# Column tiles for all products but scores, zero products in idle slots, and one of three VectorE copies on GpSimd, in a kernel of two independent parts (attention and a state-space layer)

## Chip, cores and metric

One core of one Trainium2 chip. The metric is the device time of one execution in microseconds; each kernel was run several times, and its median is quoted. The core has five engines that matter here: TensorE (PE in the profile, its weight loads are PEld), ScalarE (ACT), VectorE (DVE), GpSimd (POOL) and the DMA queues. A run counts as slow when it is over 1.5% above the fastest run of the same kernel; except where a run is said to be slow, all comparisons are of the others, the fast runs.

## The reference, cut to what matters

Two independent parts, their outputs side by side. Attention has 32 query heads of 20 dimensions and one shared key and value head, over 2048 positions. The other part is a complex diagonal recurrence with projections of 640 x 640.

```python
q = (x @ wq).reshape(B, S, H, Dh).transpose(0, 2, 1, 3)        # S = 2048, H = 32, Dh = 20
k, v = x @ wk, x @ wv
p = softmax(einsum("bhqd,bkd->bhqk", q, k) * Dh ** -0.5)
o = einsum("bhqk,bkd->bhqd", p, v)                              # then @ wo
# [...] the other part: h[t] = Lam_bar * h[t-1] + (x @ B_bar.T)[t];  y = 2 Re(h @ C.T) + x * Dskip
```

The scores are 2048 tiles of 128 keys by 512 (four heads share a row of work, 64 tiles for a block). Every tile needs an exponential, and that is what costs most: ScalarE's exponentials are the costliest group on the page of the kernel before, 802.2 us.

## The kernel before

The program contains a small scheduler that runs while the program is built. Each step has an assumed duration in ns; the scheduler plays the engines against each other with these durations and so fixes the order of each engine's instructions. On the chip the order is fixed, and the engines wait for each other by semaphores.

A score tile goes one of two ways. Most go through ScalarE: scores for three or two tiles are written to PSUM, ScalarE takes the exponential of all in one instruction. Some ("VectorE tiles") go through VectorE: it reads the scores from PSUM, and writes them as 16-bit integers whose bits, read as bf16, approximate the exponential. Four versions with different shifts (0, 32, 64, 96) are needed; the first comes from PSUM (`DR<-MB` in the profile), the other three are copies of it in SBUF with a number added (`DR<-DR`).

```python
SHIFTS = ((0, 0.24037683), (32, 0.20213201), (64, 0.16997209), (96, 0.14292892))

def score(self, op, m, out, bank):                 # one score tile: 20 dimensions and one row of bounds
    # [...]
    op.fns.append(self.mm(out, p.KT[32 * j:32 * j + 21, 128 * kc:128 * kc + 128],
                          p.QT[32 * j:32 * j + 21, qb % 2, gg, :], True, True, tile_position=(32 * j, 0)))

def fill_d(self, op, m):                           # a VectorE tile
    # [...]
    first = self.dve(self.ts(p.DR[:, h.index, 0, :], bank.ap, 16256.0, 0.0, ALU.add, ALU.max), 600, deps=[op], ...)
    for k, (sh, _) in enumerate(self.SHIFTS):
        if k:
            o = self.dve(self.ts(p.DR[:, h.index, k, :], p.DR[:, h.index, 0, :], float(sh), None, ALU.add), 200,
                         deps=[first], ...)
        self.pvq[b][j].append((p.VS[:, k, kc, 0:32], kc, p.DR[:, h.index, k, :].bitcast(BF16), ...))
```

TensorE works in three shapes. Score products are row tiles: up to four products of 32 rows of the array each, side by side. Products of probabilities with values (`MB<-PR,VP` and `MB<-DR,VS`) are column tiles: four of 32 columns each. All others (projections, outputs) use the array whole. In the trace of before, the four column tiles near 170.05 us start 3 to 4 ns apart, three score products near 169.6 us 2 to 4 ns, and a group of four column tiles of 512 columns takes as long to the start of the next of its shape as one full product does: 216 ns at full clock. GpSimd does almost nothing once the constants are made: 32 copies `rdX<-rdT`, which spread out the reciprocals of the softmax sums.

Of the kernel before, what the change touches and what calls it, by code (L numbers as in the profile page):

```python
# [20 lines left out]
class Op:  # L21
# [3 lines left out]
                 "seq", "land", "dma_key", "idx", "tail")  # L25

    def __init__(self, eng, fns, dur, deps=(), prio=5, reads=(), writes=(), prev=None, gate=None, hook=None,
                 dma_key=None, land=0.0, tail=0.0):
        self.eng, self.fns, self.dur = eng, list(fns), dur
        self.deps, self.prio, self.prev = list(deps), prio, prev  # L30
        self.reads, self.writes = list(reads), list(writes)
        self.gate, self.hook = gate, hook
        self.dma_key, self.land, self.tail = dma_key, land, tail
        self.start = self.end = None
        self.seq = self.idx = 0


class Schedule:
# [7 lines left out]
    OWN = {"pe": 0.0, "act": 60.0, "dve": 55.0, "pool": 100.0}  # L46
    URGENT = 1.0

    def __init__(self):
        self.t = 0.0  # L50
        self.pending = {e: [] for e in self.ENGINES}
        self.free = {e: 0.0 for e in self.ENGINES}
        self.order = []
        self.events = []
        self.procs = []
        self.dma_free = {}
        self.n = 0
        self.sources = {e: [] for e in self.ENGINES}
        self.slack = {"pe": 60.0, "dve": 150.0}

# [40 lines left out]
    def begin(self, op, eng):  # L101
        if op.hook is not None:
            op.hook(op)
        op.start = self.t
        if op.dma_key is not None:
# [9 lines left out]
        for lag in (0.0, 55.0, 60.0, 100.0, 110.0, 130.0, 150.0, 200.0):  # L115
            self.at(op.end + lag)

    def pick(self, eng):
        best = None
# [3 lines left out]
        for src in self.sources[eng]:  # L123
            extra = src()
            if extra is not None:
                cands = cands + [extra]
        for op in cands:
# [5 lines left out]
            if r <= t + 1e-6:  # L133
                if best is None or (op.prio, op.seq) < (best.prio, best.seq):
                    best = op
            elif op.prio <= self.URGENT and (urgent is None or r < urgent):
                urgent = r
        if best is None:
            return None
        if urgent is not None and best.prio > self.URGENT and t + best.dur > urgent + self.slack.get(eng, 1e9):  # L140
            return None
# [203 lines left out]
class Build:  # L345
    CHUNKS = (3, 2)
    MISC = 2
    NPS = 5
    NDS = 4
    SHARE = 0.215  # L350

    SHIFTS = ((0, 0.24037683), (32, 0.20213201), (64, 0.16997209), (96, 0.14292892))

# [49 lines left out]
    def alloc(self, o):  # L403
# [9 lines left out]
        self.QT = sb(o, "QT", [128, 2, NGG, 512], BF16)  # L413
# [3 lines left out]
        self.DR = sb(o, "DR", [128, self.NDS, len(self.SHIFTS), 512], I16)  # L417
        self.WO4 = sb(o, "WO4", [128, NGG, 640], BF16)
        self.PR = sb(o, "PR", [128, self.NPS, 3, 512], BF16)
# [13 lines left out]
        self.lift = sb(o, "lift", [128, 2], FP32)  # L433
# [20 lines left out]
    def alloc_late(self, s):  # L454
        self.W = self.sb(s, "W", [128, NC, 2, 512], BF16)
        self.g = self.sb(s, "g", [128, 2, 2, 512], BF16)
        self.OT = self.sb(s, "OT", [128, 12, 512], BF16)
        self.LATE = [f"W{c}" for c in range(NC)] + [f"g{u}_{i}" for u in range(2) for i in range(2)] \
            + [f"OT{i}" for i in range(12)]


    def pe(self, fns, dur, **kw):
        return self.s.add("pe", fns, dur, **kw)
# [28 lines left out]

    def mm(self, out, lhsT, rhs, start, stop, **kw):
        return lambda e: e.matmul(out, lhsT=lhsT, rhs=rhs, start=start, stop=stop, **kw)  # L494

    @staticmethod
    def mmt(n, k=1):
        return n / 2.3 * 1.0 + 8.0 * k
# [10 lines left out]
    def program(self):  # L509
# [5 lines left out]
        self.evac_op, self.norm_op = {}, {}  # L515
# [7 lines left out]
        self.d_per = {}  # L523
# [16 lines left out]
        self.s.sources["pe"].append(self.d_source)  # L540

    def warm_source(self):

        if self.started or self.s.t > 40000.0:
# [3 lines left out]
                  deps=[self.zero_op], reads=["PR0"], writes=[self.pvbank.key], hook=self.warm_last)  # L548
# [4 lines left out]
    def constants(self):  # L553
# [19 lines left out]
        many("VP", [lambda e: e.memset(p.VP[:], 0.0), lambda e: e.memset(p.VP[:, :, 20:21], 1.0)], 500)  # L573
# [3 lines left out]
        for k, (_, c) in enumerate(self.SHIFTS):  # L577
            fns.append(lambda e, k=k: e.memset(p.VS[:, k, :, 20:21], hi[k]))
            fns.append(lambda e, k=k, c=c: e.memset(p.VS[:, k, :, 21:22], c - hi[k]))
        many("VS", fns, 250)  # L580
        many("maskM", [
# [22 lines left out]
                                               channel_multiplier=1)], 250)  # L604
        rows = self.dve(lambda e: e.tensor_reduce(out=p.lift[:, 0:1], in_=p.E1[:], axis=AX.X, op=ALU.add), 120,
# [147 lines left out]
    def qt_task(self, qb, gg, bank):  # L753
        p = self
        prev = None
        slot = qb % 2
        for c in range(NC):
# [3 lines left out]
                           prio=3, reads=[f"xbT{qb}", "wq4"], writes=[bank.key])  # L761
        dst = p.QT[:, slot, gg, :]
        key = f"QT{slot}_{gg}"
# [11 lines left out]
        if qb == 0 and gg == 0:  # L775
            for c in range(NC):
# [7 lines left out]
                          deps=[m, self.lift_op], reads=[bank.key, "lift"], writes=[key, "QTr0_0"], prio=0.4)  # L784
# [14 lines left out]
    def row_task(self, qb, half, bank):  # L799
        p = self  # L800
        slot = qb % 2
# [3 lines left out]
        fns = [self.mm(bank.tensor[0:32, bank.off:bank.off + 512], p.Mm[:, gg, :], p.aq[:, gg % 4, :], gg == ggs[0],  # L805
                       gg == ggs[-1]) for gg in ggs]
        prev = self.pe(fns, 4 * self.mmt(512), deps=[self.mm_op] + [self.qt_op[(qb, gg)][1] for gg in ggs] + bank.last,
                       prio=1.5, reads=["Mm"] + [f"aq{i}" for i in range(4)], writes=[bank.key])
# [4 lines left out]
        if qb == 0 and half == 0:  # L813
            lo, ng = 1, 3
        fns = [lambda e, j=j: e.dma_start(p.QT[32 * j + 20:32 * j + 21, slot, lo:lo + ng, :],
# [3 lines left out]
                                           reads=[f"brow{rs}"] + [f"QT{slot}_{gg}" for gg in range(lo, lo + ng)],  # L819
                                           writes=[f"QTr{slot}_{gg}" for gg in range(lo, lo + ng)], prio=0, land=500.0)  # L820
# [13 lines left out]
    def attention(self):  # L834
# [10 lines left out]
        while self.tile_n < NTILE:  # L845
# [14 lines left out]
            fill = self.pe([], self.mmt(512, 2), deps=deps, prio=0, hook=lambda op, i=i: self.fill(op, i))  # L860
            self.next_fill = fill
            k += 1

    def fill(self, op, i):
# [7 lines left out]
        extra = None  # L872
        if self.want_d():
            tiles.append(self.tile_n)
            self.tile_n += 1
            extra = min(tiles, key=lambda m: self.d_per.get((m // 64, m % 4), 0))
            tiles.remove(extra)
# [4 lines left out]
        if extra is not None:  # L882
            self.fill_d(op, extra)
        op.reads = sorted(set(op.reads))
        op.dur = self.mmt(512, len(op.fns))
        dst = p.PR[:, h.index, 0:n, :]
        ex = self.act(lambda e: e.activation(dst, t[:, 0:512 * n], ACT.Exp, scale=1.0 / UNIT), 0.833 * 512 * n + 93,  # L887
# [12 lines left out]
    def score(self, op, m, out, bank):  # L900
# [5 lines left out]
        op.fns.append(self.mm(out, p.KT[32 * j:32 * j + 21, 128 * kc:128 * kc + 128],  # L906
                              p.QT[32 * j:32 * j + 21, qb % 2, gg, :], True, True, tile_position=(32 * j, 0)))
        op.reads += [f"KT{kc // 4}", f"QT{qb % 2}_{gg}", f"QTr{qb % 2}_{gg}"]
# [3 lines left out]
    def want_d(self):  # L912
        s = self.s
        if self.tile_n >= NTILE - 8 or self.d_count + 1 > self.SHARE * (self.tile_n - 16):
            return False
        if self.d_bank() is None:
            return False
        h = self.dhold[self.ndhold % self.NDS]
        return not h.taken or (h.left == 0 and s.done(h.users))

    def d_source(self):

        f = self.next_fill
        if f is None or f.start is None and f.deps and self.d_count == 0:
            return None
        if f.start is None:
            r = self.s.ready(f)
            if r is not None and r < self.s.t + self.ALONE:
                return None
        b = self.tile_n // 64  # L930
        if not self.started or not self.want_d() or not self.block_ready(b):
# [5 lines left out]
        def hook(op):  # L937
            self.tile_n += 1
            self.fill_d(op, self.tile_n - 1)
            op.reads = sorted(set(op.reads))  # L940
        return Op("pe", [], self.mmt(512, 1), prio=0.95, hook=hook)

    next_fill = None
    ALONE = 450.0

    def d_bank(self):
        s = self.s
        for b in self.free_banks:
            if all(o.end is not None and s.seen(o, "pe") <= s.t for o in b.last):
                return b  # L950
        return None
# [6 lines left out]
    def fill_d(self, op, m):  # L958

        p = self  # L960
        bank = self.d_bank()
# [4 lines left out]
        self.d_per[(m // 64, m % 4)] = self.d_per.get((m // 64, m % 4), 0) + 1  # L966
# [4 lines left out]
        first = self.dve(self.ts(p.DR[:, h.index, 0, :], bank.ap, 16256.0, 0.0, ALU.add, ALU.max), 600, deps=[op],  # L971
                         reads=[bank.key], writes=[k0], prio=0.5)
        self.s.spawn(self.d_give(bank, first))
        for k, (sh, _) in enumerate(self.SHIFTS):
            key = f"DR{h.index}_{k}"
            o = first
            if k:
                o = self.dve(self.ts(p.DR[:, h.index, k, :], p.DR[:, h.index, 0, :], float(sh), None, ALU.add), 200,
                             deps=[first], reads=[k0], writes=[key], prio=0.55)
# [3 lines left out]
    def pv_source(self):  # L983
# [23 lines left out]
        prio = 0.9 if tight else 2.0  # L1007
        return Op("pe", [], self.mmt(512, len(group)), prio=prio, hook=lambda op: self.pv(op, b, group))
# [5 lines left out]
    def pv(self, op, b, group):  # L1014
        p = self
        bank = self.pvbank
        for j, e in group:
            lhs, kc, rhs, key, ex, h, vk = e
# [20 lines left out]
    def norm_task(self, b, bank):  # L1039
# [3 lines left out]
        ot = b % 12  # L1043
        m1 = self.pe([self.mm(bank.cols(4 * i, 4 * i + 4), src[:, 128 * i:128 * i + 128], p.E1[:], True, True)
                      for i in range(4)], 4 * 65, deps=[self.evac_op[b], self.c_op["E1"]] + bank.last, prio=1.6,
                     reads=[f"pvsb{slot}", "E1"], writes=[bank.key])

        def rc(e):
            with p.nc.allow_low_precision("bf16 reciprocal of softmax denominator"):
                return e.reciprocal(p.rdT[:, slot, :], bank.cols(0, 16))  # L1050
        r = self.dve(rc, 230, deps=[m1], reads=[bank.key], writes=[f"rdT{slot}"], prio=1.2)
        spread = bass.AP(tensor=p.rdT, offset=16 * slot, ap=[[32, 128], [1, 16], [0, 32]])
        x = self.pool(lambda e: e.tensor_copy(p.rdX[:, slot, :, :], spread), 700, deps=[r], reads=[f"rdT{slot}"],  # L1053
                      writes=[f"rdX{slot}"], prio=1)
        fns = [self.mm(bank.cols(128 * i, 128 * i + 128),
                       p.rdX[:, slot, 4 * i:4 * i + 4, :].rearrange("p j d -> p (j d)"), p.ident[:], True, True)
               for i in range(4)]
        m2 = self.pe(fns, 4 * 65, deps=[x, self.c_op["ident"]], prio=1.6, reads=[f"rdX{slot}", "ident"],
                     writes=[bank.key])
        d = self.dve(self.tt(p.OT[:, ot, :], src, bank.ap, ALU.mult), 630, deps=[m2],  # L1060
# [406 lines left out]
```

## Time and profile before

| | before |
|---|---|
| median of the runs | 985.05 us (982.81 to 987.18) |
| PE, ACT, DVE, POOL busy | 93%, 83%, 76%, 3% of the span |
| mean granted TensorE clock | 0.833 |
| VectorE tiles | 337 of 2048 |

First the busy time of the engines, and two rows of the span cut in 40 slices: the busy share of ACT in tenths (9 is 90% or more) and the clock that TensorE was granted, in tenths of full speed.

```profile
PE 908.5 (93%) x6555; PEld 262.0 (27%) x6555; DVE 741.0 (76%) x1899; ACT 813.4 (83%) x699; POOL 32.2 (3%) x66
...
ACT  3597789988777999977979999899798979688992
...
PEclk8987679966557999976969999799697868689987
```

PE looks full, but part of that is a low clock: a score product takes 385 ns at full clock and 602 at half (medians). The 52 intervals in the trace have the clock at 1.0 or at 0.5, nothing else. After the first 35 us, 321 us are at 0.5, and in the slices where the clock is at 5 or 6, ACT is mostly at 8, 7 or 6.

The chain that ended last, by engine:

```profile
PE 65%; DVE 19%; ACT 11%; issue 3%; DMA 1%; ACTq 0%; POOL 0%; POOLq 0%; DVEq 0%
```

The groups of instructions that the argument needs: line, engine, operation, out<-in, shapes and count, then busy time and mean ns of one, then the idle time before them and what ended it. "21\*128" is the part of the array that a product claims, rows by columns.

```profile
L887 ACT ACTIVATE PR<-SC 128x1536 bf16<-128x1536 f32 (+1 forms) x685 | 802.2, 1244 | 124.9 <-PE SC L494 71.8
...
L494 PE MATMUL SC<-QT,KT 21*128 21x512 bf16 x1711 | 303.7, 439 | 36.7 <-ACT PR L887 20.9
L506 DVE TENSOR_SCALAR DR<-MB 128x512 int16<-128x512 f32 x337 | 230.8, 687 | 121.7 <-PE MB L494 110.7
...
L505 DVE TENSOR_SCALAR DR<-DR 128x512 int16<-128x512 int16 x1011 | 233.5, 288 | 9.8
...
L1053 POOL COPY rdX<-rdT 128x512 bf16<-128x512 bf16 x32 | 22.3, 698 | 916.7 <-DVE rdT L1050 916.7
```

The three copies of a VectorE tile take 288 ns each, and overlap a little. In the timeline of VectorE (start, duration, both in us):

```profile
start us, us, engine line op out<-in xcount [idle before <-releaser]
405.20 0.69 DVE L506 TENSOR_SCALAR DR<-MB 128x512 int16<-128x512 f32 x1 [1.27 <-PE MB L494]
405.92 0.70 DVE L505 TENSOR_SCALAR DR<-DR 128x512 int16<-128x512 int16 x3
406.54 0.68 DVE L506 TENSOR_SCALAR DR<-MB 128x512 int16<-128x512 f32 x1
407.25 0.70 DVE L505 TENSOR_SCALAR DR<-DR 128x512 int16<-128x512 int16 x3
```

One tile is 0.69 for the step out of PSUM and 0.70 for three copies. GpSimd and VectorE did disturb each other once in a while. Here are VectorE and then GpSimd, near 622 us:

```profile
622.51 1.12 DVE L501 TENSOR_TENSOR u<-prod 128x512 bf16<-128x512 bf16 x2
```

```profile
622.65 0.71 POOL L1053 COPY rdX<-rdT 128x512 bf16<-128x512 bf16 x1 [27.84 <-DVE rdT L1050]
```

Two VectorE products that take 439 ns on average span 1.12 us: the second, begun under GpSimd's copy, took 829 ns, and the copy 706 where its median is 613.

### The profile page before, as it was taken

The page shows a single profiled execution, that of the slowest core. Times are in us where ns is not written, and L with a number is a line of the kernel's source. Part 1 is how long each engine was busy: PE and PEld are TensorE (multiplying, and loading weights), DVE is VectorE, ACT ScalarE, POOL GpSimd, SP SyncE. Part 2 cuts the span into 40 slices and gives each one's busy share as a digit, 9 for nine tenths or more (in the row PEclk, how much of TensorE's full clock was granted, in tenths as well). Part 3 has the DMA queues.
Part 4 walks back from the last instruction along what each step waited for, and adds up shares of the span by engine and source line. Part 5 has one row for each costly group of instructions (what it writes and reads, how often), then busy time and mean ns, then how long its engine had stood idle before and what let it go on. Part 6 is the DMA issues. An engine that isn't in the chain of part 4 may idle for free.

```text
span 978.6 us, 16125 instructions
## 1 busy us (share of the span) xinstructions
PE 908.5 (93%) x6555; PEld 262.0 (27%) x6555; DVE 741.0 (76%) x1899; ACT 813.4 (83%) x699; POOL 32.2 (3%) x66
## 2 busy tenths in 40 slices
PE   7889999999899999999899999989999999998997
PEld 2322222222123322222233322222332322223323
DVE  6987678978775588876956797799576868688672
ACT  3597789988777999977979999899798979688992
POOL 4000000000000000000000000000000000000000
PEclk8987679966557999976969999799697868689987
DMA  9740000000000010000000100000000000000000
GB/s 164 118 87 1 1 2 1 1 1 2 2 1 6 23 38 12 7 1 1 2 6 17 34 11 8 11 1 1 5 14 12 1 11 6 6 6 1 17 12 27
DMA packets 49147, 16.63 MB, mean 17 GB/s; under 512 B 43572, under 2 KB 49072, under 8 KB 49072
## 3 DMA queue, kind: packets, MB, share of 16 engines
q1 hardware_dynamic: 44480, 14.72, 7.1%
q10 hardware_dynamic: 4592, 0.88, 0.7%
q8 instruction: 52, 0.85, 0.4%
q14 instruction: 23, 0.19, 0.1%
HBM read 1.69 MB, written 5.24 MB: 7 GB/s over the span
## 4 chain that ended last, share of the span: by engine, by line
PE 65%; DVE 19%; ACT 11%; issue 3%; DMA 1%; ACTq 0%; POOL 0%; POOLq 0%; DVEq 0%
PE MB L494 47%; PE SC L494 18%; ACT PR L887 11%; DVE DR L506 7%; DVE DR L505 6%; DVE prod L501 1%; DMA vec<-in_A_Dskip_dram 1%; DVE pvsb L1032 1%; DVE stg L1098 1%; DVE u L501 0%; DVE g L1255 0%; DVE W L501 0%; DVE fr L506 0%; DVE QT L769 0%; ACTq L485 0%
## 5 line engine op out<-in xcount | busy, mean ns | idle before, releaser
L887 ACT ACTIVATE PR<-SC 128x1536 bf16<-128x1536 f32 (+1 forms) x685 | 802.2, 1244 | 124.9 <-PE SC L494 71.8
L494 PE MATMUL MB<-PR,VP 128*32 128x512 bf16 x1711 | 339.5, 448 | 4.4 <-DVE pvsb L1032 1.9
L494 PE MATMUL SC<-QT,KT 21*128 21x512 bf16 x1711 | 303.7, 439 | 36.7 <-ACT PR L887 20.9
L506 DVE TENSOR_SCALAR DR<-MB 128x512 int16<-128x512 f32 x337 | 230.8, 687 | 121.7 <-PE MB L494 110.7
L494 PE MATMUL MB<-DR,VS 128*32 128x512 bf16 x1348 | 311.2, 465 | 1.9 <-DVE pvsb L1032 1.6
L505 DVE TENSOR_SCALAR DR<-DR 128x512 int16<-128x512 int16 x1011 | 233.5, 288 | 9.8
L494 PE MATMUL MB<-QT,KT 21*128 21x512 bf16 x337 | 147.6, 439 | 7.3 <-DVE DR L506 4.4
L494 PEld LDWEIGHTS SC<-QT,KT 21*128 21x128 bf16 x1711 | 67.3, 93 | 291.8 <-issue 132.1
L494 PEld LDWEIGHTS MB<-PR,VP 128*32 128x32 bf16 x1711 | 73.0, 97 | 120.5 <-issue 95.6
L494 PEld LDWEIGHTS MB<-DR,VS 128*32 128x32 bf16 x1348 | 66.2, 100 | 74.3 <-issue 55.7
L494 PE MATMUL MB<-xaT,BT 128*128 128x512 bf16 x200 | 73.2, 440 | 1.6 <-DVE DR L506 1.6
L494 PE MATMUL MB<-CT,W 128*128 128x128 bf16 (+1 forms) x320 | 63.0, 313 | 0.0
L494 PE MATMUL MB<-xbT,wq 128*128 128x512 bf16 x165 | 54.8, 424 | 1.3 <-DVE QT L769 1.1
L494 PE MATMUL MB<-WO,OT 128*128 128x128 bf16 (+1 forms) x256 | 53.1, 346 | 0.7 <-DVE DR L506 0.5
L501 DVE TENSOR_TENSOR prod<-MB,Z 128x1024 bf16<-128x1024 f32 x40 | 48.4, 1211 | 6.5 <-PE MB L494 6.4
L1053 POOL COPY rdX<-rdT 128x512 bf16<-128x512 bf16 x32 | 22.3, 698 | 916.7 <-DVE rdT L1050 916.7
L1098 DVE CAST stg<-MB 128x512 bf16<-128x512 f32 x40 | 27.4, 684 | 30.9 <-PE MB L494 30.8
L494 PEld LDWEIGHTS MB<-QT,KT 21*128 21x128 bf16 x337 | 31.2, 93 | 49.3 <-DVE DR L506 20.5
L1255 DVE TENSOR_TENSOR_SCAN g<-sc,hst,u 128x512 bf16<-128x512 f32 x30 | 38.2, 1285 | 0.0
L501 DVE TENSOR_TENSOR OT<-pvsb,MB 128x512 bf16<-128x512 bf16 x32 | 21.8, 682 | 19.4 <-PE MB L494 19.3
L1032 DVE CAST pvsb<-MB 128x512 bf16<-128x512 f32 x32 | 21.9, 685 | 17.7 <-PE MB L494 17.4
L494 PEld LDWEIGHTS MB<-CT,W 128*128 128x128 bf16 x320 | 22.9, 101 | 27.7 <-issue 22.5
(100 smaller groups left out, 335.4 us busy)
## 6 DMA issues: line engine op xcount, KB each, us to landing
out_dram<-stg SPq DMA_DIRECT2D x40, 128.0 KB, 1.7
wqr<-in_B_wq_dram ACTq DMA_DIRECT2D x1, 800.0 KB, 9.9
WO<-in_B_wo_dram SPq DMA_DIRECT2D x4, 200.0 KB
QT<-brow SPq DMA_DIRECT2D x28, 4.0 KB
xaT<-in_A_x_dram SPq DMA_TRANSPOSE x15, 2.7
xbT<-in_B_x_dram SPq DMA_TRANSPOSE x10, 4.7
BT<-in_A_B_re_dram SPq DMA_TRANSPOSE x5, 3.5
BT<-in_A_B_im_dram SPq DMA_TRANSPOSE x5, 3.0
```

What stands on the lines that cost most here:

```text
L494: return lambda e: e.matmul(out, lhsT=lhsT, rhs=rhs, start=start, stop=stop, **kw)
L501: return lambda e: e.tensor_tensor(out, a, b, op)
L505: return lambda e: e.tensor_scalar(out, a, s1, None, op0=op0)
L506: return lambda e: e.tensor_scalar(out, a, s1, s2, op0=op0, op1=op1)
L887: ex = self.act(lambda e: e.activation(dst, t[:, 0:512 * n], ACT.Exp, scale=1.0 / UNIT), 0.833 * 512 * n + 93, deps=[op], reads=[b.key for ...
L1032: ev = self.dve(lambda e: e.tensor_copy(p.pvsb[:, slot, :], bank.ap), 620, deps=[op], reads=[bank.key], writes=[f"pvsb{slot}"], prio=0.6, ...
L1053: x = self.pool(lambda e: e.tensor_copy(p.rdX[:, slot, :, :], spread), 700, deps=[r], reads=[f"rdT{slot}"], writes=[f"rdX{slot}"], prio=1)
L1098: ev = self.dve(lambda e: e.tensor_copy(st, bank.ap), 620, deps=[prev], reads=[bank.key], writes=[key], prio=1.8, gate=(lambda: last.end i ...
L1255: o = self.dve(lambda e, ri=ri, init=init: e.tensor_tensor_scan(p.g[:, u, ri, :], rdec, p.u[:, ri, :], init, ALU.mult, ALU.add), 1280, dep ...
```

## The change

It means to free TensorE from changes of shape (all products but scores become column tiles), to keep its clock up (products with zeros where the plan has idle time), and to free VectorE by giving GpSimd, which is idle, one copy of three. It comes with a plan that takes 97 ns for a change of shape (in the trace of before the next group starts after 312 to 332 ns instead of 216) and prefers to stay in a shape, with larger score groups, two more buffers for ScalarE's results, and other small things. The core of the diff:

```diff
+    SWITCH, STAY = 97.0, 1.2
 [...]                                   # pick(): a change of shape adds SWITCH, and STAY to the priority number
-    NPS = 5
+    NPS = 7
-    SHARE = 0.215
+    SHARE = 0.25
+    COPIES = ("dve", "dve", "pool")
 [...]
+    QUADS = True
     def mm(self, out, lhsT, rhs, start, stop, **kw):
+        if self.quads() and lhsT.shape[-1] == 128 and not kw:
+            def four(e):
+                for j in range(4):
+                    r = e.matmul(out[32 * j:32 * j + 32], lhsT=lhsT[:, 32 * j:32 * j + 32], rhs=rhs, start=start,
+                                 stop=stop, tile_position=(0, 32 * j), skip_group_check=True)
+                return r
+            return four
 [...]
+    KEEP = 3200.0
+    def keep_source(self):               # four products with a zero tile, 256 columns, if little ran in the last 3 us
 [...]
-        op.fns.append(self.mm(out, p.KT[32 * j:32 * j + 21, 128 * kc:128 * kc + 128],
-                              p.QT[32 * j:32 * j + 21, qb % 2, gg, :], True, True, tile_position=(32 * j, 0)))
+        op.fns.append(self.mm(out, p.KT[32 * j:32 * j + 32, 128 * kc:128 * kc + 128],
+                              p.QT[32 * j:32 * j + 32, b % 12, :], True, True, tile_position=(32 * j, 0)))
 [...]
             if k:
-                o = self.dve(self.ts(p.DR[:, h.index, k, :], p.DR[:, h.index, 0, :], float(sh), None, ALU.add), 200,
-                             deps=[first], reads=[k0], writes=[key], prio=0.55)
+                eng = self.COPIES[k - 1]
+                o = self.s.add(eng, self.ts(p.DR[:, h.index, k, :], p.DR[:, h.index, 0, :], float(sh), 0.0, ALU.add, ALU.max),
+                               200 if eng == "dve" else 700, deps=[first], reads=[k0], writes=[key], prio=0.55)
```

## The prediction

> **What bounds the kernel.** Measured 985.2 us. The busy table gives PE 93%, ACT 83%, DVE 76%; the chain that ended last is 65% PE, 19% DVE, 11% ACT. But PE is full mostly because its clock is low: the granted clock, mean 0.83, alternates between 1.0 and 0.5[...]. Between 35 and 960 us some 300 us run at 0.5. Score products counted against the clock intervals: 2.49 tiles per us at full clock, 1.69 at half. In full-clock stretches (318 to 431, 520 to 632 us) ACT is 93% busy; at half (257 to 318 us) 79%. So PE bounds at half clock, ACT, closely followed by PE and DVE, at full.
>
> Starts of matmuls in the timeline: four column tiles, or one 512-column full product, take 216 ns at full clock, 400 at half; where the tile shape changes (scores, column tiles, full products) the next group starts after 312 to 332 ns, so a change costs about 100 ns. I count 1674 runs of one shape; 275 boundaries are between column tiles and full products. Weighting products by their share of the array, 3.4 us windows that stayed fast mostly held over 3450 full-array columns; those that ended fast periods under 3300.
>
> **What the change does.**
> 1. Column tiles for all products: 275 boundaries go, about 30 us of PE. Streams stay at 216 ns.[...] With the preference for staying in a shape and larger score groups, perhaps 1100 to 1250 runs remain.
> 2. Zero products in idle slots hold activity above the level at which the clock falls: the large term. At full clock throughout, before's own rates would need about 793 us for the 904 us main part: -110 us. I expect a clock of 0.93 to 0.99, so about -90.
> 3. GpSimd does one of three copies: VectorE saves about 235 of 1330 ns per VectorE tile; tiles rise from 337 to perhaps 400 to 440, each moving about 450 ns off ACT and 1.1 us onto VectorE. GpSimd needs about 0.61 us each (its rdX copies: 613 ns median). [...]in this trace a two-input VectorE product starting under an rdX copy takes 829 ns instead of 439. I expect 30 to 150 us of VectorE stalls, partly off the path.
>
> Balance at full clock, estimated: ACT 0.447 us x (2048 - d), VectorE 270 + 1.13 d, equal near d = 410: 732 us; at 93% efficiency 787, plus 80 us of start, tail and remaining slow stretches: 867 us. The 35 us before the first score and the 16 us tail do not move.
>
> **Prediction: 868 us, 830 to 912 eight times in ten. Faster by over 2%: 0.95; within 2%: 0.03; slower: 0.02.**
>
> **What would show it.** Clock above 0.93; PE busy falling to 80 to 88% though instructions rise by half; ACT highest or equal; under 1300 runs of one shape; DR<-MB count 390 to 450; GpSimd copies 0.6 to 1.0 us; some VectorE DR<-DR copies stretched from 288 ns to over 500.
>
> **What would make it wrong.** Zero products placed by a modelled schedule miss the real gaps and the clock still falls (900 to 940); [...]or larger fills let ACT run nearly gapless (830).

What no trace or run of this case shows is cut from it, at the marks: a remark on the two clock levels; a cause for the 829 ns; a rise of the narrow products from 56 ns, which was to give up to 25 us of PE back; and two of the cases that would make it wrong, one of them with 900 to 930. The sum: 732 us at the balance, 787 at 93%, 867 with the 80, put as 868. Its terms are estimates. The page of before has ACT at 802.2 us for 1711 tiles (0.469 each, where the sum has 0.447) and VectorE at 0.687 us and two copies of 0.231 for a tile, and 277 us for all else (1.13 and 270 in the sum); 93% is also ACT's busy share in the two full-clock stretches; the 80 us hold the 35 of the start and the 16 of the tail, the rest is a guess. The level in point 2 is that of the windows counted above it, under 3300 and over 3450 columns; that zero products would hold it was assumed, as before has none.

## The result, and the profile after

| | before | after |
|---|---|---|
| median | 985.05 us | 954.96 us (949.84 to 958.2) |
| granted clock | 0.833 | 0.897 |
| PE, ACT, DVE, POOL busy | 93, 83, 76, 3% | 84, 84, 84, 73% |
| VectorE tiles | 337 | 338 |
| runs of one TensorE shape | 1674 | 1335 |
| time at half clock after 35 us | 321 us | 191 us |

Runs of one shape are counted from the starts of the matmuls in the trace, in which a few may be missing.

The ratio is 0.969 (95% interval 0.964 to 0.974). (A ratio here is the mean time of one kernel's fast runs over that of the other's of the same rounds, so not quite the ratio of the medians.) It was predicted to be 0.88, so some 87 us of the gain are missing.

```profile
PE 804.6 (84%) x10913; PEld 253.7 (27%) x10913; DVE 803.2 (84%) x1565; ACT 805.2 (84%) x698; POOL 699.7 (73%) x405
...
ACT  2777988787789999898799998987999978779962
POOL 4087888785986876577877766668877877897882
PEclk8977989887789999999799998997999999769977
```

```profile
DVE 42%; PE 29%; POOL 19%; ACT 6%; issue 2%; DMA 1%; SPq 1%; POOLq 0%
DVE DR L547 27%; POOL DR L547 18%; PE MB L528 10%; PE MB L532 10%; PE SC L532 10%; ACT PR L955 6%; DVE prod L542 4%; DVE g L1332 2%; DVE pvsb L1100 1%; DVE QT L835 1%; DVE u L542 1%; DVE stg L1175 1%; POOL rdX L1121 1%; DMA xbT<-in_B_x_dram 1%; SPq L517 1%
```

```profile
L955 ACT ACTIVATE PR<-SC 128x1536 bf16<-128x1536 f32 (+1 forms) x684 | 794.0, 1263 | 111.8 <-PE MB L532 60.9
L547 POOL TENSOR_SCALAR DR<-DR 128x512 int16<-128x512 int16 x338 | 668.9, 1995 | 218.8 <-DVE DR L547 216.6
L532 PE MATMUL SC<-QT,KT 32*128 32x512 bf16 x1710 | 288.3, 417 | 43.4 <-ACT PR L955 17.1
L547 DVE TENSOR_SCALAR DR<-DR 128x512 int16<-128x512 int16 x676 | 299.9, 488 | 7.3
L547 DVE TENSOR_SCALAR DR<-MB 128x512 int16<-128x512 f32 x338 | 228.3, 682 | 92.2 <-PE MB L532 88.1
```

GpSimd, planned with 700 ns and estimated by me at 610, takes 1995 ns for a copy (never under 1911). VectorE's own two copies went from a mean of 288 to 488 ns, so the two now cost 299.9 us where three cost 233.5. (Their new second step, the maximum with zero, isn't the reason: e1 below has it too, at 288 ns.) The chain that ended last is no longer PE's: it is VectorE's and GpSimd's work on `DR`, 27 and 18%. The timeline shows a tile as before, and GpSimd beside it:

```profile
start us, us, engine line op out<-in xcount [idle before <-releaser]
...
301.02 0.69 DVE L547 TENSOR_SCALAR DR<-MB 128x512 int16<-128x512 f32 x1 [0.48 <-PE MB L532]
301.74 0.91 DVE L547 TENSOR_SCALAR DR<-DR 128x512 int16<-128x512 int16 x2
```

```profile
299.08 2.02 POOL L547 TENSOR_SCALAR DR<-DR 128x512 int16<-128x512 int16 x1
301.79 3.90 POOL L547 TENSOR_SCALAR DR<-DR 128x512 int16<-128x512 int16 x2 [0.69 <-DVE DR L547]
```

The step out of PSUM still takes 0.69. The two copies left take 0.91, more than three took before (0.70): the second began 0.16 us after GpSimd did, and took 700 ns. So VectorE saves nothing on this tile, and its copies cost more in sum. And results come late for TensorE and ScalarE (who waited for whom; us in total, times, longest):

```profile
ACT PR L955 <- PE MB L532: 60.9, 69, 4.7
...
PE MB L532 <- POOL DR L547: 33.0, 31, 3.0
...
PE MB L528 <- POOL rdX L1121: 15.6, 15, 3.2
```

### The profile page after: what moved, and what is told of

It is laid out like the page before. It is cut to its first block, busy times and chain, and to the rows that moved or that the text cites. A ratio compares the mean times of both kernels' runs of the same rounds, so it can differ in the third digit from the quotient of the medians.

```text
span 956.4 us, 25005 instructions
## 1 busy us (share of the span) xinstructions
PE 804.6 (84%) x10913; PEld 253.7 (27%) x10913; DVE 803.2 (84%) x1565; ACT 805.2 (84%) x698; POOL 699.7 (73%) x405
## 4 chain that ended last, share of the span: by engine, by line
DVE 42%; PE 29%; POOL 19%; ACT 6%; issue 2%; DMA 1%; SPq 1%; POOLq 0%
DVE DR L547 27%; POOL DR L547 18%; PE MB L528 10%; PE MB L532 10%; PE SC L532 10%; ACT PR L955 6%; DVE prod L542 4%; DVE g L1332 2%; DVE pvsb L1100 1%; DVE QT L835 1%; DVE u L542 1%; DVE stg L1175 1%; POOL rdX L1121 1%; DMA xbT<-in_B_x_dram 1%; SPq L517 1%
## 5 line engine op out<-in xcount | busy, mean ns | idle before, releaser
L547 POOL TENSOR_SCALAR DR<-DR 128x512 int16<-128x512 int16 x338 | 668.9, 1995 | 218.8 <-DVE DR L547 216.6
L532 PE MATMUL SC<-QT,KT 32*128 32x512 bf16 x1710 | 288.3, 417 | 43.4 <-ACT PR L955 17.1
L547 DVE TENSOR_SCALAR DR<-DR 128x512 int16<-128x512 int16 x676 | 299.9, 488 | 7.3
L532 PE MATMUL MB<-PR,VP 128*32 128x512 bf16 x1710 | 283.6, 416 | 25.2 <-POOL DR L547 15.9
L532 PEld LDWEIGHTS SC<-QT,KT 32*128 32x128 bf16 x1710 | 67.3, 92 | 299.6 <-ACT PR L955 161.5
L532 PE MATMUL MB<-QT,KT 32*128 32x512 bf16 x338 | 135.9, 420 | 11.1 <-DVE DR L547 3.7
L528 PE MATMUL MB<-xaT,BT 128*32 128x512 bf16 x800 | 67.0, 404 | 3.4 <-DVE DR L547 2.1
L528 PE MATMUL MB<-CT,W 128*32 128x128 bf16 (+1 forms) x1280 | 65.9, 309 | 0.7 <-DVE stg L1175 0.6
L528 PE MATMUL MB<-WO,OT 128*32 128x512 bf16 (+1 forms) x1024 | 51.2, 319 | 0.2 <-DVE DR L547 0.2
L528 PE MATMUL MB<-xbT,wq 128*32 128x512 bf16 x560 | 48.4, 419 | 2.6 <-DVE QT L835 1.1
```

The lines of the kernel that those rows point to most:

```text
L528: r = e.matmul(out[32 * j:32 * j + 32], lhsT=lhsT[:, 32 * j:32 * j + 32], rhs=rhs, start=start, stop=stop, tile_position=(0, 32 * j), skip ...
L532: return lambda e: e.matmul(out, lhsT=lhsT, rhs=rhs, start=start, stop=stop, **kw)
L547: return lambda e: e.tensor_scalar(out, a, s1, s2, op0=op0, op1=op1)
```

## The experiments

Theory A: the GpSimd copy is the lost term. B: the zero products fail and the clock falls anyway. C: my balance of ACT against VectorE was too hopeful. All kernels gave the reference's result but for e2 and e10; e9 stayed within the tolerance. Times are medians, the clock is that of the profiled run; before ran beside each and had medians of 982 to 985 us.

| run | what it is | us | ratio to before | clock | VectorE copy, mean ns |
|---|---|---|---|---|---|
| e1_dve3 | after, all copies on VectorE | 845.16 | 0.860 | 0.973 | 288 |
| e2_short | after, GpSimd copies 160 of 512 columns | 838.31 | 0.853 | 0.969 | 342 |
| e8_pool32 | after, GpSimd adds packed 32-bit integers | 916.13 | 0.933 | 0.935 | 506 |
| e9_loose | after, nobody reads GpSimd's copy | 945.22 | 0.961 | 0.915 | 407 |
| e10_late | e2 and six tiny memsets | 868.95 | 0.883 | 0.957 | 423 |
| e3_model | after, planned with 1900 ns | 904.89 | 0.919 | 0.943 | 469 |
| e12_pool_add | after, GpSimd copy with one step | 913.20 | 0.928 | 0.923 | 469 |
| e4_before_pool | before, third copy on GpSimd | 1112.17 | 1.130 | 0.764 | 536 |
| e5_dve3_nokeep | e1 without zero products | 863.32 | 0.879 | 0.935 | 289 |
| e6_dve3_full | e1 without column tiles | 861.19 | 0.875 | 0.972 | 288 |
| e7_dve3_full_nokeep | e1 without both | 876.98 | 0.892 | 0.922 | 289 |
| e11_blind | e7, plan blind to shape | 908.56 | 0.924 | 0.915 | 287 |
| e13_before32 | before, scores with 32 rows | 908.44 | 0.923 | 0.941 | |
| e14_plan21 | e7, scores with 21 rows | 943.32 (fast runs 921.85, 934.58) | 0.959 (fast runs 0.943) | 0.840 | |
| e15_nps5 | e7 with 5 buffers | 886.90 | 0.902 | 0.933 | |
| e16_task3 | e7 with the old priority | 877.56 | 0.891 | 0.936 | |

### First: is it the copy?

**e1_dve3.** Undo one part.

```diff
-    COPIES = ("dve", "dve", "pool")
+    COPIES = ("dve", "dve", "dve")
```

> The changed kernel with all three shifted copies back on VectorE (its schedule is replanned: 320 VectorE tiles instead of 338). Theory A (the GpSimd copy is the lost term: 1.98 us measured where I estimated 0.61[...]): 865 to 895 us, VectorE copies back at 285 ns, clock 0.94 or more. Rival B (the clock still falls by itself, zero products miss the gaps): 935 to 960, clock 0.88 to 0.91. Rival C (my balance of ACT and VectorE was too hopeful, whatever makes the copies): 910 to 945 with clock above 0.93.

Measured 845.16 us, better than A had asked for. Its busy times, ACT and clock rows, chain, and ACT group:

```profile
PE 753.9 (90%) x10995; PEld 249.5 (30%) x10995; DVE 710.3 (84%) x1831; ACT 794.3 (94%) x705; POOL 33.5 (4%) x67
...
ACT  2699999999989999999999999998999999999992
...
PEclk9998999999979999999999999999999999998999
...
ACT 83%; PE 9%; DVE 3%; issue 2%; SPq 1%; DMA 1%; POOLq 0%; POOL 0%
...
L955 ACT ACTIVATE PR<-SC 128x1536 bf16<-128x1536 f32 (+1 forms) x691 | 783.1, 1448 | 11.2 <-PE MB L532 6.4
```

ACT is at 9 in nearly every slice, with 11 us of idle time before 691 exponentials where after has 112: the kernel is bound by ScalarE. B falls, and so does C. This version beats both kernels by over 10%.

**e2_short.** The same order of every engine as after, with the GpSimd operation made short (and `DR` set to zero once at the start).

```diff
-  self.ts(p.DR[:, h.index, k, :],   p.DR[:, h.index, 0, :],   float(sh), 0.0, ALU.add, ALU.max)
+  self.ts(p.DR[:, h.index, k, 0:w], p.DR[:, h.index, 0, 0:w], ...)      # w = 160 on GpSimd, 512 on VectorE
```

> The changed kernel in its own order, instruction for instruction, with the GpSimd copy cut to 160 of its 512 columns (result wrong on purpose), so that it lasts about 0.65 us, near the 0.7 us that the kernel's own plan assumes. A: 870 to 900. B: 940 to 960. C: 915 to 945.

Measured 838.31 us, again under the range of A.

```profile
L957 ACT ACTIVATE PR<-SC 128x1536 bf16<-128x1536 f32 (+1 forms) x684 | 776.2, 1412 | 12.1 <-PE SC L532 6.4
L547 POOL TENSOR_SCALAR DR<-DR 128x160 int16<-128x160 int16 x338 | 286.6, 852 | 465.2 <-DVE DR L547 463.3
...
L547 DVE TENSOR_SCALAR DR<-DR 128x512 int16<-128x512 int16 x676 | 200.9, 342 | 7.2
```

With a GpSimd step of 852 ns the plan of the change works; ACT hardly waits. So column tiles, zero products and the order of the plan do not by themselves hold the changed kernel back: the long GpSimd operation in place of the short one costs 955 - 838 = 117 us. Note that even 160 columns take 852 ns.

### Second: by what does it cost?

It could be that VectorE's own copies are stretched beside GpSimd's operation (488 ns instead of 288 on average; how that comes about, no run shows), or the late result and the queue behind it. Where an expectation gave a cause for it, that is cut at the mark; the times expected stand.

**e8_pool32.** The same order, the copy as 256 additions of packed integers with a constant tile, exact.

```diff
+  self.tt(p.DR[:, h.index, k, :].bitcast(I32), p.DR[:, h.index, 0, :].bitcast(I32), p.step[:], ALU.add)   # on GpSimd
```

> The changed kernel in its own order, with the GpSimd copy made as an add of 256 packed 32-bit integers to a constant tile (exact, two inputs) instead of 512 16-bit ones. I estimate 0.7 to 1.0 us instead of 1.98. Result correct. A: 880 to 915, in step with the copy's time. B: 945 to 960. C: 920 to 945.

Measured 916.13. GpSimd's group, then VectorE's:

```profile
L543 POOL TENSOR_TENSOR DR<-DR,step 128x256 int32<-128x256 int32 x338 | 271.2, 806 | 545.5 <-DVE DR L548 543.0
```

```profile
L548 DVE TENSOR_SCALAR DR<-DR 128x512 int16<-128x512 int16 x676 | 311.7, 506 | 7.3
```

This is the sharpest comparison: same order as e2, GpSimd operations as short (806 against 852 ns), their result as early (it ended 0.92 us after the step out of PSUM, 0.93 in e2, medians), TensorE waits only 1.8 us for GpSimd, and yet 78 us more. What differs is how long VectorE's copies take: one that begins within 200 ns after a GpSimd operation takes 824 ns here (median), 405 in e2. I had expected the time to follow GpSimd's duration; between these two it goes with the stretching of VectorE's copies. (Counting what each copy takes over 288 ns, the stretching is 149 us here and 38 in e2: 111 us more of it for 78 us of time.)

**e9_loose.** GpSimd does its slow operation into a spare tile, the products read another copy.

```diff
+  fn = self.ts(p.spare[:], p.DR[:, h.index, 0, :], float(sh), 0.0, ALU.add, ALU.max)      # GpSimd
+  kk = min(k, 2)        # the fourth product reads the third version
```

> The changed kernel in its own order; GpSimd does its slow operation as before but into a spare tile that nobody reads, and the products that wanted it read the third VectorE copy (result wrong on purpose). It [...]takes away TensorE's waiting for the GpSimd result. If A works mainly through late results: 880 to 910. If mainly through VectorE's stretched copies: 935 to 950, copies still near 490 ns mean. B: 945 to 960.

Measured 945.22 with copies at 407 ns. That is in the range given for VectorE's stretched copies, though the copies were not near 490 ns, and the run is inconclusive: with nobody waiting for the copies GpSimd fell behind, and the one result of it that is still needed came late: TensorE waited 53.4 us for `rdX` (15.6 in after). It traded one wait for another.

**e10_late.** Meant as lateness without the long operation: six memsets of 16 columns before the short copy of e2.

```diff
+  fns = [lambda e, i=i: e.memset(p.spare[:, 16 * i:16 * i + 16], 0) for i in range(6)] + fns     # GpSimd
```

> The short GpSimd copy of e2 (838 us) with six tiny memsets of 16 columns before it, so that its result comes about 2 us after the VectorE step, as with the full copy[...] (result wrong on purpose). If the loss of the changed kernel (955) is [...](VectorE's own copies stretched): 838 to 865. If it is the late result and the GpSimd queue: 900 to 955. VectorE copies near 340 ns mean in both cases[...].

Measured 868.95, just above the range that I gave for VectorE's stretched copies. But the run did not make what it was made for: six memsets took 0.34 us together, and the GpSimd copy ended 1.14 us after the step out of PSUM (median), against 0.93 in e2 and 2.37 in after. TensorE waited for GpSimd only 3.3 us in all. So it says little about lateness. The copies, though (minimum, median, maximum), were not as in e2:

```profile
L548 DVE TENSOR_SCALAR DR<-DR x676: 271/395/541, 48.4 to 849.3; 128x512 int16<-128x512 int16 x169
...
L548 POOL TENSOR_SCALAR DR<-DR x338: 744/780/1672, 48.8 to 849.7; 128x160 int16<-128x160 int16 x169
```

The median VectorE copy is 395 ns instead of 295. It is the first of the two copies of a tile, beside the memsets, that takes 510 ns instead of 294 (medians): beside tiny memsets it is stretched too. My expectation of 340 ns failed. The 31 us over e2 go with stretching of 92 us instead of 38; that they come from it is argued.

**e12_pool_add.** The GpSimd copy without its second step.

```diff
-  float(sh), 0.0, ALU.add, ALU.max        # on GpSimd
+  float(sh), None, ALU.add
```

> The changed kernel in its own order with the GpSimd copy as a single add, without the maximum with zero that follows it. If the second step makes it slow: copies 0.7 to 1.3 us and 860 to 915 us. [...]they stay above 1.7 us and the time at 940 to 960.

The second range, above 1.7 us, was for another cause. The copy is between the two ranges, 1588 ns (median, against 1980); the time, 913.20 us, is in the first. The second step costs 0.39 us, but most of the time is there with one. VectorE copies 469 ns; TensorE waits 18.9 us for GpSimd.

**e3_model.** Only the plan is told the truth.

```diff
-  200 if eng == "dve" else 700
+  200 if eng == "dve" else 1900
```

> The changed kernel with the one number that its plan has for the GpSimd copy set from 700 to 1900 ns, near the measured 1980; the operation is the same, the order is replanned (329 VectorE tiles). If the loss comes from planning with a wrong duration: 860 to 890. If the operation itself [...]: 915 to 955, VectorE copies still stretched to 450 ns or more on average.

Measured 904.89, between the two ranges: 50 us of the loss come back although the operation is the same. TensorE's waits for GpSimd, and VectorE's copies:

```profile
PE MB L532 <- POOL DR L547: 3.3, 4, 2.2
...
PE MB L528 <- POOL rdX L1121: 1.2, 2, 1.1
```

```profile
L547 DVE TENSOR_SCALAR DR<-DR 128x512 int16<-128x512 int16 x658 | 279.6, 469 | 7.7
```

The copies stay stretched (469 ns), but TensorE's waits for GpSimd fall from 48.6 to 4.5 us. So the wrong duration in the plan cost about 50 us, and the stretched copies the rest, about 60 against e1; e8, which has them without lateness, agrees (71 over e1).

**e4_before_pool.** The copy alone, in the kernel before.

```diff
+  add = self.dve if k < 3 else self.pool
+  o = add(self.ts(p.DR[:, h.index, k, :], p.DR[:, h.index, 0, :], float(sh), 0.0, ALU.add, ALU.max), 200 if k < 3 else 700, ...)
```

> The kernel before with nothing changed but its third shifted copy on GpSimd (planned with 700 ns; 358 VectorE tiles instead of 337). If the copy on GpSimd does the harm by itself: 1020 to 1080, VectorE copies stretched to over 420 ns on average, GpSimd operations 1.9 to 2.0 us. If the harm needs the rest of the change: within 2% of 985.

Measured 1112.17, 13% slower than before, and worse than I expected.

```profile
PE 969.6 (87%) x6533; PEld 273.9 (25%) x6618; DVE 875.1 (79%) x1625; ACT 814.0 (73%) x690; POOL 739.2 (66%) x424
...
PEclk8876678757688979876599879955798787655986
...
L506 POOL TENSOR_SCALAR DR<-DR 128x512 int16<-128x512 int16 x358 | 707.2, 1991 | 303.9 <-DVE DR L506 302.5
...
L506 DVE TENSOR_SCALAR DR<-DR 128x512 int16<-128x512 int16 x716 | 353.1, 536 | 10.1
```

Here the harm is larger than in the change. The granted clock is lower too, 0.764 against 0.833 in before, and TensorE waits 38.4 us for VectorE's `DR` and 13.6 us for GpSimd; that the waiting lowers the clock was not shown.

### Third: where does the gain come from?

**e5_dve3_nokeep**, **e6_dve3_full** and **e7_dve3_full_nokeep**: e1 without zero products, without column tiles, without both.

```diff
-    KEEP = 3200.0          # e5, e7
+    KEEP = 0.0
-    QUADS = True           # e6, e7
+    QUADS = False
```

> All copies on VectorE (e1, 845 us) without the zero products. If they are what keeps the clock up: granted clock 0.85 to 0.92, 870 to 910 us. If not: within 1% of 845 at a clock above 0.96.

> All copies on VectorE, zero products kept, but the other products full size again instead of four column tiles (replanned: 287 VectorE tiles). If column tiles save the shape changes, some 30 us of TensorE, and with them VectorE tiles: 855 to 880, more runs of one shape than the 1331 of e1, clock as e1. If they are worth nothing: within 1% of 845.

> All copies on VectorE, no zero products, other products full size: of the change only the new plan is left (times that know about shape changes, preference for staying in a shape, larger score groups, two more probability buffers, split normalisation). If column tiles and zero products give what e5 and e6 lost to e1 (18 and 16 us), 870 to 900 at a clock of 0.90 to 0.94; then the larger part of the gain over before (about 100 us) is the plan. If the gain is in the two parts together: 930 to 985.

e5 863.32, just under its range, clock 0.935 (0.973 in e1): zero products are worth 18 us, not 90. e6 861.19 with 1514 runs of one shape and an unchanged clock (0.972): column tiles are worth 16. e7 876.98: the two nearly add up (32 us), and 108 us of gain over before remain without either. (Each is a new plan: e5 has 310 VectorE tiles, e6 287, e7 288, e1 320. How much of a difference is this was not tested.)

**e11_blind.** e7, with the plan blind to shapes.

```diff
-    SWITCH, STAY = 97.0, 1.2
+    SWITCH, STAY = 0.0, 0.0
```

> e7 with the plan made blind to shape changes again (their cost and the preference for staying set to zero; 338 VectorE tiles planned). If knowing of shape changes is what the plan gains: 930 to 990, over 1600 runs of one shape, clock near 0.85. If other parts of the plan: within 2% of e7.

Measured 908.56, 1536 runs, clock 0.915: neither expectation holds. A plan that knows the shapes gives 32 us, and 76 us are still elsewhere. Fewer changes of shape are not shown to be the reason: e16 below has some 50 runs more than e11 and takes 877.56. The blind plan also has 338 VectorE tiles against 288 in e7; what of the two plans makes the 32 us stays open.

**e13_before32** and **e14_plan21.** Nothing but the rows of the score products, in an unchanged order: before with 32, e7 with 21.

```diff
-  p.KT[32 * j:32 * j + 21, ...], p.QT[32 * j:32 * j + 21, ...]        # e13; e14 is the reverse
+  p.KT[32 * j:32 * j + 32, ...], p.QT[32 * j:32 * j + 32, ...]
```

> The kernel before in its own order with score products of 32 rows (11 of them zeros) instead of 21. If the clock follows the share of array rows that a product claims: clock from 0.83 to 0.87 or more, 930 to 970. If not: 980 to 990, clock 0.83.

> e7 in its own order with score products of 21 rows instead of 32. If rows count: clock below 0.90, 890 to 930. If not: 872 to 882, clock 0.92.

e13 took 908.44 us, better than I had hoped for: eleven rows of zeros, same instructions in the same order, and 75 us less.

```profile
PE 821.4 (91%) x6555; PEld 255.1 (28%) x6555; DVE 736.7 (82%) x1899; ACT 805.6 (89%) x699; POOL 32.3 (4%) x66
...
PEclk9998999998689999999679999999997999999987
...
PE 56%; DVE 25%; ACT 14%; issue 4%; SPq 1%; DMA 1%; POOL 0%; POOLq 0%
...
L494 PE MATMUL SC<-QT,KT 32*128 32x512 bf16 x1711 | 277.5, 401 | 43.2 <-ACT PR L887 25.4
```

The clock went from 0.833 to 0.941, and the products themselves from a mean of 439 to 401 ns. They are not faster in themselves: with 21 rows and with 32 a score product takes 385 ns at full clock and 602 at half (medians, to 1 ns); only the share of the time at full clock changed. e14 lost most of what e13 gained: its two fast runs took 922 and 935 us at clocks of 0.840 and 0.823 (four more count as slow, 941 to 955 at 0.799 to 0.818), e7's 876 to 881 at 0.922 to 0.936 (on another chip, but before took 984 to 985 on both). So in these two orders the clock goes with the rows that score products claim, even where eleven of them hold zeros. All stretches of one clock in the traces of before and after, but the one cut off at the end, last whole multiples of 3.41 us (51 and 57 of them), so I counted in windows of that length. Counting products by rows times columns claimed, the windows at whose end the clock fell had up to some 2900 full-array columns in before and 2800 in e13 (90th percentile), and those that stayed fast mostly over 3060 and 3200 (10th percentile). Counting whole strips, as I did in the prediction, gives 3280 and 2800 for the first of these, which doesn't fit together. In e14 it is 2850 by rows and 3260 by strips; but e7, where the two counts are the same, has 3240, so no sharp limit is shown. That a count by rows is the right one is argued from this; that the rows matter here is shown by the two runs.

**e15_nps5** and **e16_task3**: e7 with five buffers, and with the old priority of the other products.

```diff
-    NPS = 7
+    NPS = 5                                        # e15
-        return self.TASK if self.started else 3
+        return 3                                   # e16
```

> e7 with five buffers for ScalarE's results instead of seven (270 VectorE tiles planned). If the buffers carry the plan's gain: 910 to 960. If not: within 2% of 877.

> e7 with the old low priority for the other products (274 VectorE tiles planned), so that they fill gaps instead of going ahead of score-value products. If the priority carries the gain: 910 to 960. If not: within 2% of 877.

886.90 and 877.56 against 876.98: 10 us for the buffers, nothing for the priority (replanned with 270 and 274 VectorE tiles).

Together this is a ladder, each step from a run, though from e13 to e7 much of the plan changes at once: before 984; scores with 32 rows 908 (e13; e11, with the new plan but blind, is at 909 as well); a plan that knows shapes 877 (e7); zero products 861 (e6); column tiles 845 (e1); the GpSimd copy 955 (after).

## Why the prediction was wrong

- **What bounds the kernel: right.** Half clock for a third of the time (321 of 979 us), ACT close behind at full clock (93% busy in 318 to 431 and 520 to 632 us). e1 is what that leads to, with ACT at 94% and 83% of the chain.
- **The step that failed: "GpSimd needs about 0.61 us each (its rdX copies: 613 ns median)".** It measured 1.98 us (median). I took the duration of one operation of the same size, a bf16 copy, for another, a 16-bit integer add with a maximum. The trace of before had no such operation, and so there was no measured duration to take.
- **The catch was seen, and misplaced.** "I expect 30 to 150 us of VectorE stalls, partly off the path": VectorE's copies were stretched by 137 us in sum (what each takes over 288 ns), within the range. But they were mostly on the path: the chain has 27% of VectorE's `DR` and 18% of GpSimd's, and in e8 111 us more of stretching than in e2 cost 78 us. VectorE's 235 ns saved on a tile were not saved. I had a case of this, GpSimd coming between the two copies of a tile, under what would make it wrong, with 900 to 930; it came to 955, because the plan's 700 ns added 50 (e3, without that, is at 905).
- **"Tiles rise from 337 to perhaps 400 to 440": wrong.** 338. The plan fixes that number, and the share, raised from 0.215 to 0.25 of 2048 tiles, was not what limited it; e1 has 320 and is bound by ACT all the same.
- **"Zero products ... about -90": mis-sized.** 18 us (e5 against e1). The clock was raised mostly by the 32 rows of the score products, 0.833 to 0.941 and 75 us (e13), which I had passed over in the diff; I counted a score product as a quarter of the array though it claimed 21 rows of 128.
- **Column tiles, "about 30 us of PE": small, as predicted.** 16 us of time. The rise of the 128-column products was the author's estimate and didn't come: 56 ns as four tiles too.
- **The balance:** without the GpSimd copy I would have been too high, 868 against 845. That this lies in the predicted range of 830 to 912 is partly luck: too much credit for zero products and tiles stood in for the gain of the 32 rows, which I had not counted. ACT runs with 11 us of gaps (98.6% of its time from first to last), where I had allowed 93% for the two engines.
- **What would show it:** PE at 84% held. Runs of one shape came to 1335 (expected under 1300), the clock to 0.897 (expected over 0.93), GpSimd copies to 1.98 us (expected 0.6 to 1.0). Copies stretched to over 500 ns were there.

Left open: how the 117 us between e2 and after divide exactly, as stretching and lateness act on each other; e3 and e8 put the plan's wrong duration near 50 and the stretched copies near 60 to 70, and no run has lateness alone, since e10's result was hardly later than e2's. And why a 16-bit add with a maximum on GpSimd takes three times as long as a copy of the same size (1980 against 613 ns).

## What to carry to other kernels

Work moved to an idle engine was not free here: beside it the copies of the engine that it was to relieve went from 288 to 488 ns. So measure that one operation, in the type and form it will have, and look at what it does to its neighbour's instructions, before planning with it. The granted clock is a resource like any other: here eleven rows of zeros, which made no product longer (385 ns at full clock with 21 and with 32 rows), raised it from 0.833 to 0.941 and were worth 75 us, more than any other single measure. And when a change of several parts gains little, undo them one at a time; the best version was the change without one of its parts.

## What the traces measured of the engines

- GpSimd: a one-input 16-bit add of 512 elements took at least 1482 ns with one step (e12) and 1911 with two (after), while a bf16 copy of 512 took 613 (before, median).
- VectorE beside GpSimd: by the 32-bit add of two inputs (e8), VectorE copies begun in its first 200 ns took 824 ns and ended some 150 ns after it. By the 16-bit operation of 1.98 us (after), copies begun in its first 200 ns took about 700 ns, those begun 600 to 1400 ns into it their usual 280, those begun 1400 to 1600 ns into it 673.
- The clock: 32 instead of 21 rows raised it from 0.833 to 0.941 in an unchanged order of instructions (e13).
- A change of shape on TensorE: about 100 ns at full clock (312 to 332 instead of 216 from one group to the next, before). Four column tiles of 128 columns start every 56 ns (after), as one full product did (before).
